# Second group of a fused attention and MoE kernel: half of its first product as seven half-size products, its second product in the later groups' order, and the early PSUM pool in two

## The chip, the cores and the metric

The kernel runs on one core of a Trainium2 chip. The metric is the device time of one execution in microseconds (us), as the median of several runs. The core's engines are PE (matrix products, with PEld for its weight loads), DVE (vector), ACT (scalar functions), POOL (GpSimd) and SP, which here only issues DMAs. Each engine works through its own queue in the order in which the kernel recorded its instructions, and semaphores order them against the other engines.

## The reference

```python
# 8 batches, 8 heads, 576 positions, head size 64
r = max(q, 0); q_p = [r*cos_w, r*sin_w]; k_p likewise          # features 128
kv = einsum('bhsf,bhsd->bhfd', k_p, v);  z = k_p.sum(axis=2)
x  = (einsum('bhsf,bhfd->bhsd', q_p, kv) / (einsum('bhsf,bhf->bhs', q_p, z) + 1e-6))
x  = x.transpose(0, 2, 1, 3).reshape(4608, 512)
h  = x @ w_in            # 512 x 2048, "product one"
g  = max(0.01 * h, h)
out = g @ w_out          # 2048 x 512, "product two"
```

## The kernel before, in words

The work is cut into nine groups of 512 tokens: groups 0 to 7 are the first 512 positions of a batch, group 8 gathers the last 64 positions of all eight. For each group the kernel prepares the features of q (`q_prep`, line 519, two instructions per call, one with the cosines and one with the sines) and of k (`k_cos`, `k_sin`, lines 456 and 459, one position out of nine and four heads' pairs at a time), copies v to 16 bits (`v_pairs`, line 477), forms kv on PE (`kv_sum`, line 490), transposes q's features (by PE for the first groups, by a DMA, `q_transpose_dma`, from group 2 on), forms the numerators (`num`, line 580), divides on DVE (`den`, `rec`, `mul`), transposes x (`x_transpose`, line 558, or a DMA), and then runs the two products.

**Product one.** Groups 0 and 1 do it directly (`ffn1`, line 622, called M or h): pairs of output tiles of 128 x 512 in a PSUM tile of two banks, four 512-column matmuls per tile, and one leaky ReLU of 1024 columns on ACT (line 644). From group 2 on it is done by Strassen's scheme in Winograd's form (`ffn1s` and `ffn1e`, lines 765 and 801): a group has four units u, each with seven products P(g,u,n) of four 256-column matmuls. A unit uses three PSUM banks, A, E and B, which rotate over four banks `ps_f` (`banks`, line 757). Its chain is: products 1 and 2 go to A, 5 and 3 to E, 6, 7 and 4 to B. After product 1 the step "b" copies A to B, after 5 the step "s" copies E to the one SBUF tile `s5`, product 6 adds to B, "w" writes E = B + s5 on DVE, products 3 and 7 may then go on, "y" writes y22 = B + s5 on DVE after product 7, and product 4 adds to B after "y". Steps a, c, e, d are the four leaky ReLUs on ACT (line 822). A capital B or S puts the copy on DVE, a small letter on ACT. The scheme needs sums of w_in (`w1_sum`, line 724) and, for each group, four sums of x (`x_sum`, line 741; X1, X2, X3, X4 each build on an earlier one).

**Product two.** All groups from 1 on use the same scheme for it (`ffn2s`, line 883, called F: 28 calls of four 256-column matmuls per group; group 7 goes one level deeper, line 1028). It needs sums of w_out (`weight_sum`, line 685) and of the activations G (`g_sum`, line 835). In the groups from 2 on the products run in the order 1, 6, 2, 7, 5, 4, 3 and accumulate into three chains in PSUM (`ORDER7`, `CHAIN`). Group 1 has an order and chains of its own (`ORDER71`, `CHAIN1`, line 875): products 2 and 4 get PSUM tiles of their own, so that `result` (line 922) adds on DVE what the later groups accumulate on PE.

**Order and buffers.** The order is written out by hand in the string `PROGRAM` (lines 25 to 163): each word is one call, in the order of recording, and its last letter is the engine (D, A or P). Every engine's queue follows from it. Capacity sets the rest: `stage` has four buffers for the loads, the pools `qpp` and `qpT` two each, kp one. PSUM is split into `ps_o` (two banks), `ps_n` (one tile of two banks) and, until the first Strassen unit, `ps_h` with two tiles of two banks (line 234). At the first call of `banks` the pool `ps_h` is closed and its four banks become `ps_f`. In the kernel before this happens at group 2; the PE transposes of x for group 2 still use a `ps_h` tile. `G7` = 1 names the first group with Strassen in product two, `F7` = 2 the first with it in product one.

Of the kernel before, what the change touches and what calls it, by code (L numbers as in the profile page):

```python
# [9 lines left out]
dt = mybir.dt  # L10
# [27 lines left out]
w1_sum(1,2,D) w1_sum(1,4,D) h(0,[14.15],[0.1.2.3],h) f2(1,0,4) f2(0,0,4) w2(2,P,2,4) q(1,0,0,8,D) weight_sum(2,0,4)  # L38
q(1,1,0,8,D) q(1,2,0,8,D) q(1,3,0,8,D) w2(2,D,0,2) k(1,0,1,c,D) k(1,0,1,s,D) k(1,1,2,c,D) k(1,1,2,s,D) v(1,0,1,D)
w2(3,D,2,4) f2(2,0,4) f2(0,4,8) f2(3,0,4) f2(2,4,8) qT(1,0,A,h) qT(1,1,A,h) f2(1,4,8) f2(3,4,8) qT(1,2,A,h) f2(1,8,12)  # L40
qT(1,3,A,h) f2(2,8,12) f2(0,8,12) v(1,1,2,A) kvps(1,h) kv(1,0,2) f2(3,8,12) kvo(1,0,2,A) w2(3,D,0,2)
k(1,2,4,c,A,[0.7]) v(1,3,4,A) k(1,2,4,c,D,[7.9]) nh(1,0,0,h) kvps(1,h) nh(1,1,0,h) f2(2,12,14) den(1,0,0) k(1,2,3,s,D)
rec(1,0,0) den(1,1,0) rec(1,1,0) k(1,3,4,s,D) mul(1,0,0) mul(1,1,0) load(k,3) load(q,3) f2(2,14,16) v(1,2,3,P)
f2(3,12,16) f2(0,12,16) kv(1,2,4) f2o(2,A) f2o(3,A) kvo(1,2,4,A) q_prep(2,0,0,8,A) f2o(0,A) xh(1,0,0,h) xh(1,1,0)
f2(1,14,15) nh(1,0,1,h) xho(1,0,D) nh(1,1,1,n) f2(1,12,14) h(1,[0.1],[0.1],h) den(1,0,1) den(1,1,1) rec(1,0,1)
mul(1,0,1) rec(1,1,1) mul(1,1,1) xh(1,0,1,o) xho(1,1,A,0,1) h(1,[2.3],[0.1],h) q_prep(2,2,0,8,D) k_sin(2,6,P)
xh(1,1,1) h(1,[4.5],[0.1],n) f2(1,15,16) xho(1,1,A,1,2) k_cos(2,8,A) f2o(1,A) h(1,[0.1.2.3.4.5],[2.3]) M(1,6) M(1,7)
M(1,8) M(1,9) M(1,10) k_cos(2,0,D) k_sin(2,4,D) q_prep(2,1,0,8,D) weight_sum(1,4,8) k_cos(2,2,D) k_cos(2,1,D)
q_prep(2,3,0,8,D) k_cos(2,5,P) k_cos(2,3,D) v_pairs(2,2,4,D) k_sin(2,8,D) k_sin(2,5,P) k_sin(2,3,P) w1_sum(0,3,D)
# [1311 lines left out]
```

## Time and profile before

| | |
|---|---|
| median of 3 runs | 269.49 us (269.48 to 272.55) |
| the profiled execution | 270.13 us |
| its span, first to last instruction | 268.1 us |
| granted TensorE clock | 1.00 throughout |
| DVE, ACT, POOL busy over the span | 83%, 69%, 42% |
| HBM read, written | 36.70 MB, 9.44 MB |

The span is 2.0 us shorter than the execution that it was taken from. In the profile, PE's instructions are pipelined: a 256-column matmul is shown with about 0.27 us although the next one starts 0.11 us later, so a busy share near 100% says only that PE always had something in its pipe. How fast it goes is read from the distance between the starts.

### The profile page before, as it was taken

Reading aid. Unit: us, or ns where it says so; the run is one execution under the profiler, and the core shown is the slowest. Engines: PE = TensorE matmul, PEld = TensorE weight load, DVE = VectorE, ACT = ScalarE, POOL = GpSimd, SP = SyncE. Lnnn points to the kernel's source line nnn. Section 1 sums busy time; section 2 is a strip of 40 time slices with the busy share of each in tenths; the row PEclk is TensorE's granted clock in tenths of the full one; section 3 lists DMA queues with packets and bytes.
Section 4 is the critical chain, followed back from the end, with each engine's and each line's share of the span. In section 5 each row is a group of like instructions: output and inputs, shape, how many; then the busy total and the mean of one; then the engine's idle time right before and its main releaser. Section 6 shows DMA issues by size and latency. Waiting matters only on the chain.

```text
span 268.1 us, 7401 instructions
## 1 busy us (share of the span) xinstructions
PE 261.7 (98%) x3009; PEld 223.1 (83%) x3009; DVE 222.9 (83%) x480; ACT 185.8 (69%) x336; POOL 113.5 (42%) x101
## 2 busy tenths in 40 slices
PE   8899999999999999999999999999999999999994
PEld 3675455656899999899999999999999999999983
DVE  4853899898989888799679799878798989998983
ACT  7866438778968988698896577886656376476610
POOL 2468011422838941090191369941461031354530
PEclk9999999999999999999999999999999999999999
DMA  7999999999999599979999899772756043100075
GB/s 231 363 394 412 382 398 373 391 255 210 265 241 348 108 243 208 366 174 247 238 325 182 141 355 250 180 111 51 142 134 143 18 76 122 41 0 2 2 236 156
DMA packets 75041, 57.09 MB, mean 213 GB/s; under 512 B 47232, under 2 KB 63616, under 8 KB 74624
## 3 DMA queue, kind: packets, MB, share of 16 engines
q1 hardware_dynamic: 74400, 56.11, 75.5%
q10 hardware_dynamic: 608, 0.52, 0.6%
q8 instruction: 23, 0.38, 0.5%
q14 instruction: 10, 0.08, 0.1%
HBM read 36.70 MB, written 9.44 MB: 172 GB/s over the span
## 4 chain that ended last, share of the span: by engine, by line
PE 85%; DMA 5%; ACT 4%; SPq 2%; POOL 1%; issue 1%; DVE 1%; ACTq 0%
PE ps_f L790 30%; PE ps L909 26%; PE ps_h L633 10%; PE ps_o L657 5%; DMA vst<-in_v_dram 3%; PE ps_kv L502 2%; PE ps L1061 2%; ACT qp L425 2%; DMA out_dram<-osb 2%; PE ps_num L586 2%; PE ps_y L1061 2%; PE ps_f L909 1%; SPq L539 1%; ACT vm L433 1%; PE ps_xT L1210 1%; PE ps_kv L1161 1%
## 5 line engine op out<-in xcount | busy, mean ns | idle before, releaser
L822 ACT ACTIVATE G<-ps_f 128x512 f16<-128x512 f32 x84 | 48.5, 597 | 30.5 <-PE ps_f L790 28.0
L909 PE MATMUL ps<-w,G 128*128 128x256 f16 x432 | 59.3, 273 | 0.0
L909 PEld LDWEIGHTS <-G 128*128 128x128 f16 x560 | 53.5, 98 | 5.6
L790 PE MATMUL ps_f<-xT,w 128*128 128x256 f16 x336 | 49.2, 273 | 0.0
L790 PEld LDWEIGHTS <-w 128*128 128x128 f16 x448 | 48.0, 114 | 0.9
L790 PEld LDWEIGHTS <-wsum 128*128 128x128 f16 x336 | 36.6, 114 | 0.9 <-issue 0.5
L909 PE MATMUL ps<-T,ext 128*128 128x256 f16 x208 | 29.6, 272 | 0.0
L633 PE MATMUL ps_h<-xT,w 128*128 128x512 f16 (+1 forms) x144 | 29.1, 355 | 0.0
L427 POOL TENSOR_SCALAR kp<-kst,sin_t 128x256 f16<-128x256 f32 x17 | 21.4, 1266 | 11.0 <-PE ps_kv L502 6.2
L790 PE MATMUL ps_f<-X,wsum 128*128 128x256 f16 x176 | 25.8, 273 | 0.0
L633 PEld LDWEIGHTS <-w 128*128 128x128 f16 x144 | 15.9, 114 | 10.9
L683 DVE TENSOR_TENSOR ps_f<-ps_f,s 128x512 f32<-128x512 f32 x28 | 19.5, 697 | 6.3 <-ACT s L433 3.8
L909 PEld LDWEIGHTS <-ext 128*128 128x128 f16 x224 | 21.4, 98 | 2.2
L644 ACT ACTIVATE G<-ps_h 128x1024 f16<-128x1024 f32 x16 | 15.9, 1022 | 7.2 <-PE ps_h L633 7.2
L683 DVE TENSOR_TENSOR y<-ps_f,s 128x512 f32<-128x512 f32 x28 | 19.2, 685 | 1.9 <-PE ps_f L790 1.5
L610 DVE TENSOR_TENSOR xs<-ps_num,rden 128x512 f16<-128x512 f32 x28 | 19.3, 688 | 0.7
L427 POOL TENSOR_SCALAR qp<-qst,cos_t 128x512 f16<-128x512 f32 (+1 forms) x5 | 9.5, 1892 | 23.6 <-DMA qpT<-qp 19.3
L822 ACT ACTIVATE G<-y 128x512 f16<-128x512 f32 x28 | 17.7, 632 | 0.8 <-DVE y L683 0.8
L433 ACT COPY ps_f<-ps_f 128x512 f32<-128x512 f32 x27 | 15.6, 579 | 3.1 <-PE ps_f L790 2.4
L790 PE MATMUL ps_f<-X,w 128*128 128x256 f16 x112 | 16.8, 273 | 0.0
L790 PE MATMUL ps_f<-xT,wsum 128*128 128x256 f16 x112 | 16.8, 273 | 0.0
L683 DVE TENSOR_TENSOR osb<-ps,ext 128x512 f32<-128x512 f32 x20 | 13.6, 683 | 2.3 <-PE ps L909 2.1
(171 smaller groups left out, 527.2 us busy)
## 6 DMA issues: line engine op xcount, KB each, us to landing
qst<-in_q_dram SPq DMA_DIRECT2D x7, 1024.0 KB, 10.2
out_dram<-osb SPq DMA_DIRECT2D x28, 256.0 KB, 4.6
kst<-in_k_dram SPq DMA_DIRECT2D x5, 1152.0 KB, 7.2
vst<-in_v_dram SPq DMA_DIRECT2D x5, 1152.0 KB, 9.0
w2st<-in_moe_w_out_dram SPq DMA_DIRECT2D x3, 1024.0 KB, 13.3
vst<-in_v_dram SPq DMA_DIRECT2D x4, 576.0 KB, 7.1
ext<-in_moe_w_in_dram SPq DMA_DIRECT2D x4, 512.0 KB, 11.2
kst<-in_k_dram SPq DMA_DIRECT2D x2, 576.0 KB, 7.8
```

What stands on the lines that cost most here:

```text
L425: nc.scalar.activation(o, i, AF.Relu, scale=col)
L427: eng.tensor_scalar(out=o, in0=i, scalar1=0.0, scalar2=col, op0=ALU.max, op1=ALU.mult)
L433: nc.scalar.copy(o, i)
L610: nc.vector.tensor_tensor(out=xs(), in0=ps[:, :, 0 : 4 * NE].rearrange("p a (b e) -> p a b e", e=NE)[:, :, :, 0:D], in1=st["rden", *k].rea ...
L633: nc.tensor.matmul(ps[:, m % 2, lo:hi], lhsT=w1[m // 4, c][0][:, w1[m // 4, c][1], m % 4 : 512 : 4], rhs=xT[:, lo // P : hi // P, c, :], s ...
L644: nc.scalar.activation(st["g", g][:, m - 1 : m + 1, :], ps, AF.Lrelu)
L657: nc.tensor.matmul(st["ps_o", g, tt], lhsT=st["g", g][:, m, tt * P : (tt + 1) * P], rhs=w2[:, m, :], start=(m == 0), stop=(m == NFT - 1),)
L683: eng.tensor_tensor(out=o, in0=a, in1=b, op=op)
L790: nc.tensor.matmul(ps[:, mi * HT : (mi + 1) * HT], lhsT=a[:, c, 2 * r0 + mi : 512 : 4], rhs=b[:, c], start=(n in (1, 5) and mi == 0 and c ...
L822: nc.scalar.activation(st["g", g][:, m : m + 2, r * HT : (r + 1) * HT], {"a": A, "c": y22, "e": E, "d": B_}[e].rearrange("p (m t) -> p m t ...
L909: nc.tensor.matmul(ps[:, tt], lhsT=a[:, i, tt * P : (tt + 1) * P], rhs=b[:, i], start=(first and i == 4 * halves[0]), stop=(i == NPR - 1 a ...
L1061: nc.tensor.matmul(ps, lhsT=a[:, i], rhs=b[:, i], start=(fresh and i == 0), stop=(i == NI - 1), skip_group_check=True,)
```

## The change

In group 1 the first half of product one (tiles 0 to 7, the calls `h`) stays direct. The second half, tiles 8 to 15 (`M(1,8)` to `M(1,15)`), becomes the units u = 2 and u = 3 of the Strassen scheme: P(1,2,n), P(1,3,n) with their steps e(1,2,.) and e(1,3,.). For these, x sums X1 to X4 of group 1 are formed (`x_sum(1,..)`), and the sums of w_in's second half are complete earlier (`w1_sum(1,3)`). `F7` is now compared with the running unit 4g + u, and is 6.

Product two of group 1 loses its own order and chains and takes those of the later groups: `R(1,2)` is a copy on ACT and no sum on DVE any more.

The pool `ps_h` becomes two pools of one tile each, chosen by a list of 26 digits (`H_BUF`), so that each half of the four `ps_f` banks takes the place of one of them. The transposes of x for group 2 write to two `ps_f` banks.

`PROGRAM` is written anew from the second group to the middle of group 4. The first difference comes after `f2(1,0,4) f2(0,0,4)`, from about unit 1 of group 4 on the words are nearly, and from `kv_sum(6,0,4,n)` on exactly, as before. In the new part the casts `w2(3,..)` of the last quarter of w_out move from DVE to ACT, `v(1,1,2)` from ACT to DVE, `v(1,3,4)` and `q_prep(2,1)` and more of `k_cos`/`k_sin` to POOL, and the loads `k(3)` and `q(3)` are recorded later.

```diff
-    F7 = 2
+    F7 = 6
...
-    early = ExitStack()
-    ps_h = early.enter_context(tc.tile_pool(name="ps_h", bufs=2, space=PS))
+    early = [ExitStack() for _ in range(2)]
+    ps_h = [
+        early[i].enter_context(tc.tile_pool(name=f"ps_h{i}", bufs=1, space=PS))
+        for i in range(2)
+    ]
+    taken = []
+    H_BUF = [int(i) for i in "01010110101010110100110101"]
...
-            early.close()
-            ps_f = pool("ps_f", 1, PS)
-            st["H"] = [ps_f.tile([P, 512], dt.float32, name=f"ps_f{i}") for i in range(4)]
+            for i in (1, 0):
+                early[i].close()
+            st["H"] = []
+            for i in range(2):
+                ps_f = pool(f"ps_f{i}", 1, PS)
+                st["H"] += [ps_f.tile([P, 512], dt.float32, name=f"ps_f{2 * i + j}") for j in range(2)]
...
-            st["ps_x", g] = psum("h", [P, 2, J // 2, NKC, P], dt.float16, "ps_x")
-        ps = st["ps_x", g][:, j % 2, j // 2]
+        ps = st["H"][(12 * g + 2 + j % 2) % 4].bitcast(dt.float16).rearrange(
+            "p (j c t) -> p j c t", j=J // 2, c=NKC
+        )[:, j // 2]
...
-    ORDER71 = (1, 2, 6, 5, 7, 4, 3)
-    CHAIN1 = {**CHAIN, 2: "W", 4: "V"}
...
-        lone, last = g == G7, g == NG - 1
-        order, chain = (ORDER71, CHAIN1) if lone else (ORDER79, CHAIN9) if last else (ORDER7, CHAIN)
+        last = g == NG - 1
+        order, chain = (ORDER79, CHAIN9) if last else (ORDER7, CHAIN)
```

The words of `PROGRAM` around the new units, before and after:

```diff
-xh(1,1,1) h(1,[4.5],[0.1],n) f2(1,15,16) xho(1,1,A,1,2) k_cos(2,8,A) f2o(1,A) h(1,[0.1.2.3.4.5],[2.3]) M(1,6) M(1,7)
-M(1,8) M(1,9) M(1,10) k_cos(2,0,D) k_sin(2,4,D) q_prep(2,1,0,8,D) weight_sum(1,4,8) k_cos(2,2,D) k_cos(2,1,D)
...
+h(1,[4.5],[2.3]) h(1,[0.1.2.3],[2.3]) f2(1,15,16) P(1,2,1) P(1,2,5) k_sin(2,5,D) e(1,2,b) k_sin(2,0,A) k_cos(2,8,P)
+k_cos(2,1,P) k_cos(2,6,A) x_sum(1,2,D) k_sin(2,4,P) k_sin(2,2,D) k_sin(2,3,A) h(1,[6.7],[0.1.2.3],n) weight_sum(4)
+k_cos(2,5,D) q_prep(2,3,0,8,D) k_sin(2,7,D) weight_sum(3) e(1,2,S) P(1,2,6) x_sum(1,4,D) e(1,2,w) P(1,2,2) P(1,3,1)
+e(1,2,a) x_sum(1,3,D) P(1,2,3) P(1,2,7) e(1,2,e) e(1,3,b) g_sum(1,1,0,4) e(1,2,y) P(1,3,5) g_sum(1,2,0,4) F(1,0)
+e(1,3,s) P(1,3,6) e(1,3,w) v_pairs(2,2,4,D) P(1,3,2) P(1,2,4) e(1,2,c) f2o(1,A) k_cos(2,0,A) k_cos(2,3,A) e(1,3,a)
+P(1,3,7) load(k,3) load(q,3) q_transpose_dma(2,0) P(1,3,3) F(1,2) k_cos(2,7,P) k_cos(2,4,P) k_sin(2,8,P)
+v_pairs(2,0,2,P) e(1,3,y) k_sin(2,1,D) q_prep(3,0,0,8,D) P(1,3,4) e(1,3,c) e(1,3,e) e(1,2,d) e(1,3,d) kv_sum(2,0,4,n)
```

How this moves the instructions, at three places. Rows read: line, operation, out<-in, shape; `xN` merges equal neighbours, "..." leaves rows out (on PE, the weight load ahead of every matmul and the other three matmuls of the same four). Lines of the changed kernel are some 10 to 20 higher: its 645 and 807 are 633 and 790 of the kernel before.

**PE, the second half of group 1's product one.** Before, where tiles 8 to 15 are made:

```order
L633 MATMUL ps_h<-xT,w_2_0_101 128x512
...
L633 MATMUL ps_h<-xT,w_2_2_102 128x512
...
L633 MATMUL ps_h<-xT,w_3_0_103 128x512
...
L633 MATMUL ps_h<-xT,w_3_2_104 128x512
...
L502 MATMUL ps_kv<-vm,kp 128x66
```

After, from the last of the direct tiles 6 and 7 on (933, 934, 938, 939 are the four banks; these rows are P(1,2,6), P(1,2,2), P(1,3,1), P(1,2,3), P(1,2,7), P(1,3,5)):

```order
L645 MATMUL ps_h<-xT,w_1_2_103 128x512
...
L807 MATMUL ps_f_938<-X_183,wsum 128x256
...
L807 MATMUL ps_f_933<-xT,w_2_2_105 128x256
...
L807 MATMUL ps_f_939<-xT,w_2_0_104 128x256
...
L807 MATMUL ps_f_934<-xT,wsum 128x256
...
L807 MATMUL ps_f_938<-xT,w_3_0_106 128x256
...
L807 MATMUL ps_f_933<-X1b,wsum 128x256
```

Between product 6 and product 3 of unit 2 stand three groups of four 256-column matmuls (product 6 itself, 2, and product 1 of unit 3), where before there were only direct tiles, which wait for no sum.

**ACT, the same place.** Before:

```order
L433 COPY osb<-ps_o 128x512
L644 ACTIVATE G_96<-ps_h 128x1024 x6
L425 ACTIVATE kp<-kst,cos_t 128x4x64 x2
L425 ACTIVATE kp<-kst,sin_t 128x4x64
L644 ACTIVATE G_96<-ps_h 128x1024 x2
L509 CAST kv_171<-ps_kv 128x2x4x66
```

After (the COPY rows are the steps b of units 2 and 3 and s of unit 3):

```order
L656 ACTIVATE G_99<-ps_h 128x1024 x3
L444 COPY ps_f_938<-ps_f_933 128x512
L436 ACTIVATE kp<-kst,sin_t 128x4x64
L436 ACTIVATE kp<-kst,cos_t 128x4x64
L436 ACTIVATE kp<-kst,sin_t 128x4x64
L656 ACTIVATE G_99<-ps_h 128x1024
L839 ACTIVATE G_99<-ps_f_933 128x2x256
L839 ACTIVATE G_99<-ps_f_934 128x2x256
L444 COPY ps_f_934<-ps_f_939 128x512
L444 COPY s_186<-ps_f_933 128x512
L839 ACTIVATE G_99<-y_187 128x2x256
```

Three leaky ReLUs of 1024 columns in a row now stand ahead of the first step of unit 2, and the second of them frees the tile whose banks product 1 of unit 2 writes.

**DVE, between the last division of group 1 and kv_sum of group 2.** Before:

```order
L427 TENSOR_SCALAR qp<-qst,cos_t 128x8x64
L427 TENSOR_SCALAR qp<-qst,sin_t 128x8x64
L683 TENSOR_TENSOR T_177<-w_105 128x1024
L427 TENSOR_SCALAR kp<-kst,cos_t 128x4x64 x2
L427 TENSOR_SCALAR qp<-qst,cos_t 128x8x64
L427 TENSOR_SCALAR qp<-qst,sin_t 128x8x64
L427 TENSOR_SCALAR kp<-kst,cos_t 128x4x64
L435 CAST vm<-vst 128x18x64
```

After (X1b, X_183 and X_184 are X1, X2 and X4 of group 1; the COPY is step s of unit 2, the row with ps_f_934 its step w):

```order
L695 TENSOR_TENSOR X_183<-xT,X1b 128x512
L438 TENSOR_SCALAR kp<-kst,sin_t 128x4x64
L695 TENSOR_TENSOR ext<-w_108,T_181 128x2048
L438 TENSOR_SCALAR kp<-kst,cos_t 128x4x64
L438 TENSOR_SCALAR qp<-qst,cos_t 128x8x64
L438 TENSOR_SCALAR qp<-qst,sin_t 128x8x64
L438 TENSOR_SCALAR kp<-kst,sin_t 128x4x64
L695 TENSOR_TENSOR w_108<-w_108 128x8x256
L446 COPY s_186<-ps_f_934 128x512
L695 TENSOR_TENSOR X_184<-xT,X_183 128x512
L695 TENSOR_TENSOR ps_f_934<-ps_f_938,s_186 128x512
L695 TENSOR_TENSOR xT<-xT 128x2x2x128
```

The steps s and w, for which PE waits, now stand behind two sums of 2048 columns, and the sum of x for product 7 (the last row) behind w.

More of the change, by code (lines that the diff above doesn't have):

```diff
@@ L742, in x_sum @@
         need(("xT", g), *(("X", g, i) for i in {1: (), 2: (1,), 4: (2,), 3: (1,)}[n]))
-        if g > F7 and n in (2, 4):
+        if g == 1 and n == 3:
+            need(*(("f1", 1, m) for m in range(8)))
+        if g > 1 and n in (2, 4):
             need(("f1", g - 1, "product", {2: 6, 4: 4}[n]))
@@ L1217, in xT_ho @@
         done.update(("xTc", b, 2 * hg + c, j) for c in range(*cs) for j in range(2 * lo, 2 * hi))
+        if all(("xTc", b, c, j) in done for c in range(NKC) for j in range(J)):
+            done.add(("xT", b))
         copy(
```

143 lines of the change are left out of this document (71 added, 72 removed).

## The prediction

> **What bounds the kernel now.** First the page, for which engine the end hangs on.
>
> ```profile
> PE 261.7 (98%) x3009; PEld 223.1 (83%) x3009; DVE 222.9 (83%) x480; ACT 185.8 (69%) x336; POOL 113.5 (42%) x101
> PE   8899999999999999999999999999999999999994
> PEclk9999999999999999999999999999999999999999
> PE 85%; DMA 5%; ACT 4%; SPq 2%; POOL 1%; issue 1%; DVE 1%; ACTq 0%
> ```
>
> PE has something in its pipe in every slice from the third to the last but one, at full granted clock, and the chain that ended last runs through it for 85% of the span. A time can come only out of the number of columns that PE passes, or out of holes between its matmuls. For these I read the timeline of PE around the change, by starts.
>
> ```profile
> 40.57 1.89 PE L657 MATMUL ps_o<-w,G 128*128 128x512 f16 x8
> 52.47 0.38 PE L657 MATMUL ps_o<-w,G 128*128 128x512 f16 x1
> 52.68 11.39 PE L633 MATMUL ps_h<-xT,w 128*128 128x512 f16 x52
> 64.00 1.32 PE L502 MATMUL ps_kv<-vm,kp 64*128 64x66 f16 x72
> ...
> 73.24 0.42 PE L586 MATMUL ps_num<-kv,qpT 128*128 128x66 f16 x8
> 73.72 0.38 PE L565 MATMUL ps_x<-ident,xs 128*128 128x128 f16 x4
> ...
> 92.55 0.60 PE L790 MATMUL ps_f<-X,w 128*128 128x256 f16 x4
> 92.99 0.60 PE L790 MATMUL ps_f<-xT,w 128*128 128x256 f16 x4
> 93.43 0.60 PE L790 MATMUL ps_f<-xT,wsum 128*128 128x256 f16 x4
> 93.86 0.60 PE L909 MATMUL ps<-w,G 128*128 128x256 f16 x4
> 94.43 0.60 PE L790 MATMUL ps_f<-X,w 128*128 128x256 f16 x4
> ...
> 109.87 0.42 PE L586 MATMUL ps_num<-kv,qpT 128*128 128x66 f16 x8
> 110.13 0.60 PE L909 MATMUL ps<-w,G 128*128 128x256 f16 x4
> 111.03 0.60 PE L790 MATMUL ps_f<-X1b,wsum 128*128 128x256 f16 x4 [0.30 <-ACT G L822]
> ```
>
> Eight 512-column matmuls take 1.89 us with a tail of 0.38 for the last: (1.89 - 0.38) / 7 = 0.216 us each. Four 256-column ones take 0.44 from start to start (92.55, 92.99, 93.43): 0.110 each. Against these rates there are three holes in the part that is written anew: 0.22 at 73.72 (eight num matmuls need 0.26, as from 109.87 to 110.13), 0.13 at 94.43, 0.46 at 111.03: together 0.81 us. The 52 direct matmuls run without one. The part of the kernel that is rewritten is thus nearly full, and PE bounds it.
>
> **The change part by part.** *Columns.* Tiles 8 to 15 cost 8 x 4 = 32 matmuls of 512 columns, 32 x 0.216 = 6.91 us. The two units cost 2 x 7 x 4 = 56 of 256 columns, 56 x 0.110 = 6.16. Gain **0.75 us**. Product two has 28 x 4 matmuls of 256 columns in either order, and kv, num and the transposes stay, so no other column is saved.
>
> *The wait of unit 2 for its banks.* Product 1 needs the tile of `h` 0 and 1 to be read by ACT. Tiles 4 and 5 are done first, then 0 and 1, then 2 and 3, in steps of four matmuls, 0.86 us; behind them comes one f2 matmul (0.22), then product 1. In the rows of the timeline and of the page
>
> ```profile
> 53.80 2.85 ACT L644 ACTIVATE G<-ps_h 128x1024 f16<-128x1024 f32 x3 [0.33 <-PE ps_h L633]
> ...
> L644 ACT ACTIVATE G<-ps_h 128x1024 f16<-128x1024 f32 x16 | 15.9, 1022 | 7.2 <-PE ps_h L633 7.2
> ```
>
> three leaky ReLUs take 2.85, of which one alone is 1.02 long, so they follow each other at 0.92. With the tail of the matmul (0.38 - 0.22 = 0.16) and a hand-over of 0.1, the first begins 0.26 after tiles 4 and 5, and the second ends at 0.26 + 0.92 + 1.02 = 2.20; PE reaches product 1 at 0.86 + 0.86 + 0.22 = 1.94. **+0.3 us**; bounds 0 (if the hand-overs cost nothing) and 0.6 (a k_sin of ACT in front is late by 0.3).
>
> *The chain inside the units.* What a step of the chain costs is shown at 92.99, where PE waits for y:
>
> ```profile
> 93.68 0.69 DVE L683 TENSOR_TENSOR y<-ps_f,s 128x512 f32<-128x512 f32 x1 [0.30 <-ACT kp L425]
> ```
>
> Product 7 starts at 92.99 and ends at 93.59, y runs from 93.68 to 94.37, product 4 starts at 94.43: 1.44 us from a product to the one that needs its sum, and PE was held up by it (the hole of 0.13). In the new order of PE twelve matmuls of 256 columns, 12 x 0.110 = 1.32, stand from product 6 to product 3 in unit 2, from 6 to 7 in unit 3, and from 7 to 4 in unit 3. Each lacks 0.12: **+0.4 us** with rounding. In the later groups other work stands between; here the only other work is eight matmuls of F(1,0) and F(1,2).
>
> *DVE ahead of step w.* The steps s and w of unit 2 stand behind the preparation of group 2.
>
> ```profile
> 50.95 0.48 DVE L427 TENSOR_SCALAR qp<-qst,cos_t 128x512 f16<-128x512 f32 x1
> 51.35 0.61 DVE L427 TENSOR_SCALAR qp<-qst,sin_t 128x512 f16<-128x512 f32 x1
> 51.88 0.56 DVE L427 TENSOR_SCALAR kp<-kst,cos_t 128x256 f16<-128x256 f32 x1
> 52.35 0.34 DVE L427 TENSOR_SCALAR kp<-kst,sin_t 128x256 f16<-128x256 f32 x1
> 52.62 0.62 DVE L427 TENSOR_SCALAR qp<-qst,cos_t 128x512 f16<-128x512 f32 x1
> 53.16 0.69 DVE L427 TENSOR_SCALAR qp<-qst,sin_t 128x512 f16<-128x512 f32 x1
> ...
> 59.23 1.21 DVE L683 TENSOR_TENSOR ext<-w,T 128x2048 f16<-128x2048 f16 x1
> 60.37 0.75 DVE L435 CAST vm<-vst 128x1152 f16<-128x1152 f32 x1
> ...
> 52.94 2.52 POOL L427 TENSOR_SCALAR kp<-kst,sin_t 128x256 f16<-128x256 f32 x2
> ```
>
> Beside POOL (busy here until 55.46) a half q takes 0.40 to 0.61 from start to start, say 0.52, and a k 0.27 to 0.47, say 0.37. A sum of 2048 columns takes 1.14 (59.23 to 60.37). From 51.1 on DVE has four halves of q (2.1), five k (1.85), two sums of x (0.35 each by the estimate of half a 1024-column sum, 0.7), two sums of 2048 (2.3) and then s (0.6, an estimate by half of the 1.21 above) and X4 (0.35): it is free for w at 59.0. PE comes to product 1 of unit 2 in the row order at 55.7 and ends product 6 at 55.7 + 0.44 + 0.44 + 8 x 0.216 + 0.60 = 58.9, so w could start at 59.0: **0 us**, but with no reserve. Bounds: 0, and 0.9 if every q and k goes at the slowest rate shown (0.61 and 0.47).
>
> *kv of group 1.* v(1,1) moves from ACT to DVE.
>
> ```profile
> 41.45 0.74 DVE L435 CAST vm<-ext 128x576 f16<-128x576 f32 x1
> 42.40 0.74 PE L1161 MATMUL ps_kv<-vm,kp 64*128 64x66 f16 x36
> ```
>
> DVE had its cast and one k (0.67) to 42.1; the second cast then ends at 42.85, while the second half of the 36 matmuls would start at 42.74: **+0.15 us** (bounds 0 and 0.4). In return ACT casts two quarters of w_out, which DVE does now:
>
> ```profile
> 42.11 1.28 DVE L435 CAST w<-ext 128x1024 f16<-128x1024 f32 x2
> ...
> 40.77 1.01 ACT L433 COPY qpT<-ps_qt 128x1024 f16<-128x1024 f16 x1 [0.25 <-PE ps_qt L575]
> ```
>
> No row shows ACT at it; the nearest is its copy of 1024 columns, 1.01, which I take (0.64 to 1.3 each otherwise, DVE's rate and POOL's 1.29 in the row further below). The second ends about 44.7, and f2 of these rows is reached at 45.0; it is hidden, and would cost what it is late beyond that.
>
> *Moved with cover.* R(1,2) becomes a copy on ACT for a sum on DVE, where ACT, with 8.36 us of 15.5 in the row of rival B, has room; the x transposes and product two's new chains have the same matmuls. On SP the loads of k(3) and q(3) keep their place in the queue; v(3)'s first half now stands between the two transposes of group 2's q, of which the second waits for q_prep(2,3) as the load does. More of k(2) is on POOL, whose work for group 2 I put at 12.5 us (11.71 in that same row, and a little more); from 47.4 on it ends near 60, before kv_sum(2) at about 64. All this costs nothing as long as these reserves stand.
>
> *Holes elsewhere.* The three holes of 0.81 us go with the old order; the new one up to group 4 is packed as closely, so I put in the same 0.81 for its own (bounds 0 and 2).
>
> Sum: -0.75 + 0.3 + 0.4 + 0 + 0.15 - 0.81 + 0.81 = **+0.1 us**: the span goes from 268.1 to 268.2. The profiled execution is 270.13 us and the median 269.49; the difference added to the median gives **269.6 us**.
>
> **The rivals.** *(A) The columns come through.* The waits in the units are hidden by what PE has queued, the holes of the old order vanish: -0.75 - 0.81 + 0.4 = -1.2, 268.3 us. For it speaks that the old order shows 52 matmuls without a hole and only 0.81 us in 50 us; against it, that the chain of 1.44 is longer than 1.32 on paper already.
>
> *(B) DVE takes over the bound in the new units (slower).* From the moment DVE reaches step w later than 59.0, each microsecond passes to PE undiminished, since eight matmuls (0.88 us) are all that does not depend on the units before kv_sum(2), which needs DVE's last k too. With 0.9 from the slow rates, 0.6 at the banks and 0.4 at kv, and 0.4 in the chain: -0.75 + 2.3 = +1.55, 271.0 us. DVE's 14.8 busy of 15.5 us in this stretch speak for it:
>
> ```profile
> 48.50:64.00 15.50, 15.50 (x92) 8.36 (x91) 14.84 (x34) 11.71 (x17) 4.93 (x4) 1.00 1.02 280
> ```
>
> against it, that w_out's last casts (1.28 us) leave DVE ahead of them and POOL takes three of the k and a q.
>
> *(C) POOL shuts DVE out.* One row shows a DVE instruction that waits for the whole of a POOL one:
>
> ```profile
> 35.90 1.29 POOL L435 CAST w<-w2st 128x1024 f16<-128x1024 f32 x1 [9.43 <-DMA w2st<-in_moe_w_out_dram]
> 36.20 1.26 DVE L427 TENSOR_SCALAR qp<-qst,sin_t 128x512 f16<-128x512 f32 x1
> ```
>
> 0.48 became 1.26. If each of the 13 DVE instructions ahead of s met this beside POOL's 12.5 us, at half of 0.8 to 1.2 each, w would be 6 us late: 269.6 + 6 = 275.6 us. Against it speaks that the six rows from 50.95 on, all beside POOL, lost some 0.8 us together, not 0.8 each. The Trainium skill ("SBUF — State Buffer", Who interferes with whom) states this as a rule: the port pair that DVE and GpSimd share is locked for the whole instruction, and the second one fully blocks. The trace agrees in the one row and not in the six.
>
> *(D) The columns saved don't reach the end*, because something else than PE sets it: then the time stays at 269.5 plus the waits only, 270.3. A PE at 98% leaves little room for it.
>
> **How the numbers follow.** Forecast, near balance, 0.55; A 0.22; B 0.16; C 0.03; D 0.04. The likeliest is 269.6 us. The range must hold A but for a little (to 268.2) and B with a worse packing later on (271.0 + 0.9 = 271.9); C and the rest of A lie outside: **268.2 to 271.9**. A change of 2% (5.4 us), about what a measurement of this kernel can tell from no change, would need on the fast side several times the 1.56 us that columns and holes hold: 0.01. On the slow side only C reaches it: 0.03. Within 2%: 0.96.
>
> **What would show it right or wrong.** Right: 24 more matmuls; product 1 of unit 2 some 0.3 us late behind the second leaky ReLU; 1.44 from product 6 to 3 in unit 2; DVE reaching w within 0.3 us of the end of product 6; kv of group 1 with a gap of 0.15 in its middle; from group 4 on the same distances as before. Wrong: a hole of over 1 us anywhere in PE between 50 and 130 us, above all ahead of product 3 of unit 2 (B or C), at kv_sum(2) (POOL or DVE late with k), or at num of group 2 (transposes late); or no hole at all in the units (A).

## The result, and the profile after

The changed kernel takes **271.8 us** (median of 20 runs, 270.52 to 273.1) against 269.73 us for the kernel before in the same sessions (20 runs). The ratio is **1.0061, 95% interval 1.004 to 1.0082**: slower by 1.1 to 2.2 us, far below 2%. The forecast was 269.6 us with a range of 268.2 to 271.9: the time lies 0.1 us inside the upper end, and a change of +0.1 us had been forecast where +2.1 came. The profiled execution took 272.29 us, its span is 270.5 us. The page, as before by engine and by the chain that ended last:

```profile
PE 261.5 (97%) x3033; PEld 225.1 (83%) x3033; DVE 226.2 (84%) x474; ACT 187.6 (69%) x341; POOL 133.2 (49%) x115
PE 77%; DMA 11%; DVE 6%; SPq 2%; issue 1%; ACT 1%; DVEq 0%
```

PE is busy as long as before (261.5 for 261.7) with 24 more, shorter matmuls, but the chain now runs through it for 77% and not 85%: 6% go through DVE and 11% through DMAs. POOL has 20 us more work. The units, in the timeline of PE:

```profile
55.20 0.38 PE L669 MATMUL ps_o<-w,G 128*128 128x512 f16 x1
55.71 0.60 PE L807 MATMUL ps_f<-xT,w 128*128 128x256 f16 x4
...
58.31 0.60 PE L807 MATMUL ps_f<-X,wsum 128*128 128x256 f16 x4
58.75 1.04 PE L807 MATMUL ps_f<-xT,w 128*128 128x256 f16 x8
59.86 0.60 PE L807 MATMUL ps_f<-xT,wsum 128*128 128x256 f16 x4
...
61.16 0.60 PE L919 MATMUL ps<-w,G 128*128 128x256 f16 x4
61.74 0.60 PE L807 MATMUL ps_f<-X,wsum 128*128 128x256 f16 x4
...
62.62 0.60 PE L807 MATMUL ps_f<-X,w 128*128 128x256 f16 x4
63.20 0.60 PE L807 MATMUL ps_f<-xT,w 128*128 128x256 f16 x4
...
64.07 0.60 PE L919 MATMUL ps<-w,G 128*128 128x256 f16 x4
64.63 0.60 PE L807 MATMUL ps_f<-X,w 128*128 128x256 f16 x4
```

Four matmuls of 256 columns need 0.44 from start to start, one of 512 needs 0.22; what is more is a hole. They are: 0.30 at 55.71 (product 1 of unit 2), 0.24 at 59.86 (product 3), 0.14 at 61.74 (product 6 of unit 3), 0.15 at 63.20 (product 7) and 0.13 at 64.63 (product 4), together 0.95 us, where the direct tiles had none. Further on there are 0.57 us at 72.74 (num of group 2) and 0.41 at 95.76 (product 1 of group 3).

The rest of the accounting uses four marks of PE that both programs share: an early matmul of group 1's product one (PE's number 470, counted from 0; before at 49.86, after at 50.01), the first matmul of kv_sum of groups 2 and 6, and PE's end. All values in us; "again" is the changed kernel profiled a second time.

| stretch | before | after | again |
|---|---|---|---|
| to matmul 470 | 49.86 | 50.01 | 49.96 |
| 470 to kv_sum 2 | 14.14 | 15.16 | 15.05 |
| kv_sum 2 to kv_sum 6 | 82.09 | 82.15 | 82.10 |
| kv_sum 6 to PE's end | 118.22 | 118.23 | 118.23 |
| PE's end to the span's end | 3.82 | 4.95 | 4.41 |

The second stretch of after holds eight more matmuls of product two (0.88), which its third stretch lacks. Taken together, 470 to PE's end is 1.09 us longer (0.93 again), the span's tail 1.13 (0.59 again). The part from kv_sum 6 on is the same to 0.02 us in all 14 profiles of this study. So there are two losses: one between 50 and 147 us, one behind PE's last matmul; 0.15 (0.10 again) stand ahead of matmul 470.

### The profile page after: what moved, and what is told of

It is laid out like the page before. It is cut to its first block, busy times and chain, and to the rows that moved or that the text cites. A ratio compares the mean times of both kernels' runs of the same rounds, so it can differ in the third digit from the quotient of the medians.

```text
span 270.5 us, 7473 instructions
## 1 busy us (share of the span) xinstructions
PE 261.5 (97%) x3033; PEld 225.1 (83%) x3033; DVE 226.2 (84%) x474; ACT 187.6 (69%) x341; POOL 133.2 (49%) x115
## 4 chain that ended last, share of the span: by engine, by line
PE 77%; DMA 11%; DVE 6%; SPq 2%; issue 1%; ACT 1%; DVEq 0%
PE ps_f L807 31%; PE ps L919 29%; DMA w2st<-in_moe_w_out_dram 5%; DMA w1st<-in_moe_w_in_dram 4%; PE ps_o L669 4%; PE ps_kv L513 3%; PE ps_num L598 3%; PE ps L1071 2%; DMA xT<-xs 2%; PE ps_y L1071 2%; PE ps_f L919 1%; DVE qp L438 1%; DVE kp L438 1%; SPq L314 1%; PE ps_qt L587 1%
## 5 line engine op out<-in xcount | busy, mean ns | idle before, releaser
L839 ACT ACTIVATE G<-ps_f 128x512 f16<-128x512 f32 x90 | 52.3, 596 | 32.8 <-PE ps_f L807 31.3
L807 PE MATMUL ps_f<-xT,w 128*128 128x256 f16 x360 | 52.1, 273 | 0.4 <-DMA xT<-xs 0.2
L807 PEld LDWEIGHTS <-wsum 128*128 128x128 f16 x360 | 39.1, 113 | 1.0 <-issue 0.2
L807 PE MATMUL ps_f<-X,wsum 128*128 128x256 f16 x184 | 27.1, 272 | 0.0
L438 POOL TENSOR_SCALAR kp<-kst,cos_t 128x256 f16<-128x256 f32 (+1 forms) x19 | 22.6, 1199 | 8.4 <-ACT G L839 4.4
L438 POOL TENSOR_SCALAR qp<-qst,cos_t 128x512 f16<-128x512 f32 (+1 forms) x7 | 14.0, 2007 | 24.3 <-DMA qpT<-qp 18.4
L695 DVE TENSOR_TENSOR ps_f<-ps_f,s 128x512 f32<-128x512 f32 x30 | 20.9, 695 | 5.7 <-ACT s L444 2.9
L645 PE MATMUL ps_h<-xT,w 128*128 128x512 f16 (+1 forms) x112 | 22.2, 348 | 0.0
L438 POOL TENSOR_SCALAR kp<-kst,sin_t 128x256 f16<-128x256 f32 x13 | 15.7, 1208 | 0.0
L656 ACT ACTIVATE G<-ps_h 128x1024 f16<-128x1024 f32 x12 | 11.9, 1023 | 5.5 <-PE ps_h L645 4.6
```

The source lines that it names most:

```text
L438: eng.tensor_scalar(out=o, in0=i, scalar1=0.0, scalar2=col, op0=ALU.max, op1=ALU.mult)
L645: nc.tensor.matmul(ps[:, m % 2, lo:hi], lhsT=w1[m // 4, c][0][:, w1[m // 4, c][1], m % 4 : 512 : 4], rhs=xT[:, lo // P : hi // P, c, :], s ...
L656: nc.scalar.activation(st["g", g][:, m - 1 : m + 1, :], ps, AF.Lrelu)
L695: eng.tensor_tensor(out=o, in0=a, in1=b, op=op)
L807: nc.tensor.matmul(ps[:, mi * HT : (mi + 1) * HT], lhsT=a[:, c, 2 * r0 + mi : 512 : 4], rhs=b[:, c], start=(n in (1, 5) and mi == 0 and c ...
L839: nc.scalar.activation(st["g", g][:, m : m + 2, r * HT : (r + 1) * HT], {"a": A, "c": y22, "e": E, "d": B_}[e].rearrange("p (m t) -> p m t ...
```

## The experiments

Theory H: the saved columns are paid back by local holes in the new order, each of which can be had back. Theory D: DVE with POOL beside it is full, so a hole that is closed opens again elsewhere. Expectations are quoted as they stood before each run. "470 to end" is the third and fourth marks' distance on PE: 214.45 us before, 215.54 and 215.38 after. This mark moves by some tenths from one profile to the next: before_pad, whose program is that of the kernel before up to 198 us, gives 214.04. A difference under 0.4 us is therefore read from the hole that went or came, and not from the mark alone. Diffs show words of `PROGRAM`; the numbers in brackets are the 95% interval of the ratio to the kernel before.

**again**: nothing altered.

> The changed kernel once more, nothing altered, for the spread and as the base of the others. Theory H (holes of the new order): the same holes in PE at the same places as in the first profile, 0.30 at product 1 of unit 2, 0.24 at its product 3, 0.57 at num of group 2, 0.41 at product 1 of group 3, and the end of PE 1.2 us later than before; the time 1.2 to 2.3 us above the kernel before. Theory J (the loss is a jitter of DMAs and of the output at the end): the holes stand elsewhere, and the end of PE is within 0.4 us of that of the kernel before.

Measured: 1.0069 (1.0045 to 1.0093). The holes stand at the same places (0.30, 0.14 at product 3, 0.14, 0.15, 0.13; 0.57; 0.50), PE ends 1.03 us later than before. The loss is no accident of one run; theory J is out for PE.

**bank**: PE gets other work while the banks come free.

```diff
-f2(1,15,16) P(1,2,1) P(1,2,5) ... h(1,[6.7],[0.1.2.3],n)
+f2(1,15,16) h(1,[6.7],[0.1],n) P(1,2,1) P(1,2,5) ... h(1,[6.7],[2.3],n)
```

> Four matmuls of tiles 6 and 7 are moved ahead of product 1 of unit 2, so that PE has 0.86 us of other work while the second leaky ReLU frees the banks. Theory H in its simple form: the 0.30 us hole goes and the end of PE comes 0.3 us earlier. Theory D: DVE reaches step w of unit 2 at the same time as now (it is busy until 0.2 us behind product 6 already), so product 3 starts where it started and its hole grows from 0.24 to some 0.54: no gain, under 0.1 us.

```profile
55.32 0.81 PE L645 MATMUL ps_h<-xT,w 128*128 128x512 f16 x3
55.97 0.60 PE L807 MATMUL ps_f<-xT,w 128*128 128x256 f16 x4
...
58.14 1.04 PE L807 MATMUL ps_f<-xT,w 128*128 128x256 f16 x8
59.15 0.60 PE L807 MATMUL ps_f<-xT,wsum 128*128 128x256 f16 x4
```

Product 1 follows the matmul ahead of it at once (three need 0.65), and the hole at product 3 did not grow: 59.15 - 58.14 - 0.88 = 0.13 (0.14 in again). From 470 to kv_sum 2 it takes 14.76 for 15.05 of again: the 0.30 is gained, theory H is right here. To PE's end it gains 0.65 in this one profile. The time does not show it: 1.0081 (1.0053 to 1.0108).

**bank_dve**: DVE's order ahead of the steps s and w of unit 2.

```diff
-weight_sum(3) e(1,2,S) P(1,2,6) x_sum(1,4,D) e(1,2,w) ... e(1,2,y)
+e(1,2,S) P(1,2,6) e(1,2,w) x_sum(1,4,D) ... e(1,2,y) weight_sum(3)
```

> As the run before it, and on DVE the sum of 2048 columns for product two (1.21 us) goes from ahead of steps s and w of unit 2 to behind step y, and the sum of x for product 4 from ahead of w to behind it. Theory D for this place (the new units wait for DVE's other work): w starts 0.1 us behind product 6, the bank hole and half of the hole at product 3 are gone: the end of PE 0.4 us earlier than in the changed kernel. Theory H without DVE: the same 0.3 us as the run before it brought, no more.

The timeline of DVE and PE around unit 3:

```profile
63.77 1.22 DVE L695 TENSOR_TENSOR w<-w 128x2048 f16<-128x2048 f16 x1
...
64.71 0.60 PE L807 MATMUL ps_f<-X,w 128*128 128x256 f16 x4
...
65.51 0.69 DVE L695 TENSOR_TENSOR ps_f<-ps_f,s 128x512 f32<-128x512 f32 x1
...
66.25 0.60 PE L807 MATMUL ps_f<-xT,w 128*128 128x256 f16 x4 [0.94 <-DVE ps_f L695]
```

Neither expectation held for PE's end. At unit 2, w does start 0.1 us behind product 6 (61.12 for 61.02), as theory D had it; but in bank, with the sum of 1.21 us still ahead of it, w also starts 0.1 us behind product 6 (58.40 for 58.30), so the sum had cost nothing there. Now it stands ahead of unit 3's w and makes that w 1.1 us late: product 7 starts at 66.25 where 65.15 would do. 470 to kv_sum 2 is 15.80, a microsecond more than bank. So it depends on the place what DVE can hide: the whole sum ahead of unit 2's w, next to nothing of it ahead of unit 3's. (This run also lost 2.7 us ahead of matmul 470, where no row differs from bank; its k tile landed at 9.53 us and not at 7.88. That part is not the experiment's, so the ratio, 1.014 (1.0113 to 1.0168), is no measure of it.)

**num_first**: two k features behind the division for which num waits.

```diff
-den(2,1) k_cos(3,1,D) k_sin(3,6,D) rec(2,1) mul(2,1)
+den(2,1) rec(2,1) mul(2,1) k_cos(3,1,D) k_sin(3,6,D)
```

> Two k features of group 3 on DVE are moved behind the reciprocal and the product of group 2's second quarter, for which num of the third quarter waits. Theory H: the 0.57 us hole ahead of that num shrinks to 0.1 or less and the end of PE comes 0.4 to 0.5 us earlier than in the unaltered changed kernel. Theory D (DVE as a whole is the bound): the k features come 1 us later, their wait turns up at kv_sum of group 3 or at the next division, and the end moves by less than 0.15 us. Theory J: no effect on the time beyond the spread.

In the changed kernel the features stand between `den` and `mul`, and num's tile is free only after `mul`:

```profile
70.65 0.15 DVE L608 TENSOR_SCALAR den<-ps_num 128x8 f32<-128x8 f32 x1
...
70.72 0.56 DVE L438 TENSOR_SCALAR kp<-G,cos_t 128x256 f16<-128x256 f32 x1
71.20 0.56 DVE L438 TENSOR_SCALAR kp<-G,sin_t 128x256 f16<-128x256 f32 x1
...
71.90 0.69 DVE L622 TENSOR_TENSOR xs<-ps_num,rden 128x512 f16<-128x512 f32 x1
...
72.74 0.41 PE L598 MATMUL ps_num<-kv,qpT 128*128 128x66 f16 x8 [0.40 <-DVE xs L622]
```

With them behind, that hole goes, and the next num waits 0.52 us:

```profile
75.16 0.43 PE L598 MATMUL ps_num<-kv,qpT 128*128 128x66 f16 x8 [0.35 <-DVE xs L622]
```

kv_sum 2 to kv_sum 3 is 13.08 for 13.04: theory D. 470 to end is 215.93, more than before the mend, and the ratio 1.008 (1.005 to 1.0109), because further on the mechanism of the prediction's rival C appeared:

```profile
115.44 2.24 POOL L446 CAST vm<-vst 128x1152 f16<-128x1152 f32 x2
...
115.64 2.58 DVE L695 TENSOR_TENSOR G<-G,ext 128x1024 f16<-128x1024 f16 x1
...
119.70 0.49 PE L807 MATMUL ps_f<-xT,w 128*128 128x256 f16 x3 [0.53 <-DVE ps_f L695]
```

A sum that takes 0.68 took 2.58: DVE came 0.2 us behind POOL and got nothing until both of POOL's casts were done. s, w and product 7 behind it were late, 0.70 us on PE. In again the same sum came 0.45 us ahead of the casts, and had its 0.68, although a feature was running on POOL from 0.64 us ahead of it to 0.50 behind its start:

```profile
115.78 0.68 DVE L695 TENSOR_TENSOR G<-G,ext 128x1024 f16<-128x1024 f16 x1
116.23 2.33 POOL L446 CAST vm<-vst 128x1152 f16<-128x1152 f32 x2
```

**num_act**: the two features leave DVE for ACT, a third goes behind a division.

```diff
-den(2,1) k_cos(3,1,D) k_sin(3,6,D) rec(2,1) mul(2,1) ... k_cos(3,8,D) mul(2,2) ... R(1,2,A)
+den(2,1) rec(2,1) mul(2,1) ... mul(2,2) k_cos(3,8,D) ... R(1,2,A) k_cos(3,1,A) k_sin(3,6,A)
```

> The two k features of group 3 that stood on DVE ahead of the division of group 2's second quarter go to ACT, into its idle 1.3 us there, and a third one on DVE goes behind the division of the third quarter. Theory D (DVE is the bound between kv_sum of group 2 and kv_sum of group 3, so that work must leave it): the hole of 0.57 at num goes and none of 0.5 takes its place as it did at the next quarter when the features were only put later; kv_sum of group 3 comes 0.45 to 0.6 us earlier. Theory H in its local form (each hole by itself): the same gain, but the next quarter shows its 0.5 us hole again, as no order of ACT's work bears on it.

```profile
72.31 0.42 PE L598 MATMUL ps_num<-kv,qpT 128*128 128x66 f16 x8
...
74.97 0.42 PE L598 MATMUL ps_num<-kv,qpT 128*128 128x66 f16 x8
```

Measured: no hole at either num (the rows name no wait); kv_sum 2 to kv_sum 3 is 12.44 for 13.04, 470 to end 214.51, and 1.0057 (1.0031 to 1.0084). Theory D: putting DVE's work later brought nothing, taking it off DVE brought 0.60. Between matmul 470 and PE's end this kernel is now as fast as the one before (214.45), and its time is still 1.5 us longer: in its profile, what is left of the span's loss lies ahead of matmul 470 (0.39) and behind PE's end (0.63).

**p30**: other products fill the hole ahead of product 1 of group 3.

```diff
-P(3,0,1) ... P(2,3,4) P(3,0,5) ... P(3,0,6) ... F(2,1) F(2,2) P(3,1,1)
+P(2,3,4) P(3,0,1) ... P(3,0,5) F(2,2) ... P(3,0,6) ... F(2,1) P(3,1,1)
```

> Product 4 of the last unit of group 2 is put ahead of product 1 of group 3, and a product-two step of four matmuls behind product 5 of group 3. Theory H (the hole of 0.31 to 0.50 there is the landing of group 3's x transpose): product 4 fills most of it; what is left is 0.2 ahead of product 4 (step y ends 0.3 behind the matmul ahead), and the end of PE comes 0.2 to 0.35 us earlier. Rival (the x transpose is not what PE waits for): a hole of 0.3 to 0.5 stands again ahead of product 1 or product 6 of group 3, no gain.

What PE waits for there, in the chain of waits of the changed kernel, is the DMA of group 3's x transpose:

```profile
89.08 0.49 ACT s L444
89.57 0.01 issue
89.58 6.14 DMA xT<-xs
95.72 0.05 issue
95.76 0.30 PE ps_f L807
```

And with the products moved:

```profile
94.73 0.60 PE L919 MATMUL ps<-w,G 128*128 128x256 f16 x4
95.30 0.60 PE L807 MATMUL ps_f<-X,w 128*128 128x256 f16 x4
95.73 0.60 PE L807 MATMUL ps_f<-xT,w 128*128 128x256 f16 x4
...
98.35 0.60 PE L807 MATMUL ps_f<-xT,w 128*128 128x256 f16 x4
99.29 0.60 PE L807 MATMUL ps_f<-xT,w 128*128 128x256 f16 x4 [0.34 <-DVE ps_f L695]
```

The hole shrank to 0.13, ahead of product 4, and product 1 of group 3 (95.73) follows with none: the x transpose was what PE waited for, against the rival. But a hole of 0.50 opened at 99.29, behind step w, where the filler had been taken from. 470 to end is 215.54: no gain, as the rival had it, for another reason than the rival's. The ratio was 1.0118 (1.0065 to 1.0171, four runs).

**direct** and **direct2**: the units alone undone.

```diff
-P(1,2,n) P(1,3,n) e(1,2,.) e(1,3,.) x_sum(1,n,D) ... w1_sum(1,3,D)
+M(1,8) M(1,9) ... M(1,14) M(1,15) ... w1_sum(1,3,D) behind kv_sum(2,0,4,n)
-F7 = 6
+F7 = 8
```

> The units alone undone: in the changed kernel, tiles 8 to 15 of group 1 are direct again (32 matmuls of 512 columns, leaky ReLUs of 1024 columns on ACT, no x sums and no steps of group 1), all else of the change stays: product two in the later order, the split PSUM pools, the work moved between engines. Measured at the end of PE against the changed kernel. Theory H (columns gained are paid back by the stalls inside the units): columns +0.81, the stalls inside the units of 0.65 go, the wait of 0.30 for the first bank stays with the first direct tile: +0.15, between -0.1 and +0.4. Theory D (the units' cost is their 5 us of DVE, which make num of group 2 and the k features late): the hole of 0.57 at num of group 2 closes as well, -0.4. Theory A (the saved columns come through, the loss is only in the rest): +0.8.

> The units alone undone, as in the run named direct, but with the copy and two k features on ACT ahead of the last pair of direct tiles in ACT's queue; there they stood behind its leaky ReLU, and kv_sum of group 2 waited 1.7 us for them. From PE's matmul 470 to its end, against 215.4 in the changed kernel: theory H (columns +0.81, stalls inside the units -0.65): 215.4 to 215.7, no difference worth a measurement; theory A (the columns of the units come through): 216.1 or more; theory D (the units' DVE work is what makes num late): 214.8 or less.

In direct, kv_sum 2 waited 1.7 us for k features that I had left behind a leaky ReLU on ACT, so it tells nothing of the units (1.0105, 1.0076 to 1.0134). In direct2 470 to end is 215.71, 0.2 to 0.3 more than with the units: within theory H, but no more than the mark moves by itself. Its time is 1.0056 (1.0036 to 1.0076), not to be told from the changed kernel's. Three larger holes stand in it, without any unit (0.30, 0.68 and 0.54 us):

```profile
55.10 0.38 PE L669 MATMUL ps_o<-w,G 128*128 128x512 f16 x1
55.61 7.07 PE L645 MATMUL ps_h<-xT,w 128*128 128x512 f16 x32
...
68.71 1.05 PE L919 MATMUL ps<-T,ext 128*128 128x256 f16 x8 [0.52 <-DVE ext L695]
...
73.44 0.41 PE L598 MATMUL ps_num<-kv,qpT 128*128 128x66 f16 x8 [0.37 <-DVE xs L622]
```

The first is the bank wait, now ahead of the first direct tile: it belongs to the order and not to the units. The second is direct2's own: the sum `w1_sum(1,3)`, put back behind kv_sum 2, stands on DVE ahead of the sum that product two waits for. So the units are best read up to kv_sum 2, ahead of both other holes: 15.31 us for 15.16 (15.05 again). The units gain 0.15 to 0.25 there, which is their columns (0.81) less the holes in their chain (0.66, 0.55).

**direct_num**: direct2 with the words of num_act.

> As direct2, and the k features moved as in num_act. Theory H: the same 0.6 to 0.9 us as num_act brought to the changed kernel: 214.6 to 215.0 from matmul 470 to the end, and since this kernel has so few ACT instructions that none is the 448th, the span ends 3.8 us behind PE; time 0.3 to 0.9 us above the kernel before. Rival (the hole at num comes from the units): the gain is under 0.3.

Measured: 215.19 (0.52 less than direct2; kv_sum 2 to kv_sum 3 takes 13.13 for 13.70) and 1.0035 (1.0018 to 1.0052), the lowest of the changed kernels. The gain is a little under H's 0.6 and above the rival's 0.3: the hole at num does not come from the units. Against num_act, which has the units and the same mend at num, PE's part is 0.68 longer (215.19 for 214.51), as much as the hole that direct_num keeps from direct2 (0.68), and the tail 0.66 shorter (3.79 for 4.45).

**pad** and **before_pad**: the tail.

```diff
+pad=lambda n: [nc.scalar.activation(warm, zero, AF.Lrelu) for _ in range(n)],
+pad(12) qT(1,2,A,h)
```

in pad, and in the kernel before

```diff
-e(6,2,c)
+e(6,2,c) pad(9)
```

> The changed kernel with 12 ACT instructions on one column each, in an idle time of ACT about 38 us, so that every later ACT instruction stands 12 further in the program. In the four profiles with the changed program's ACT queue the last output DMA on ACT is issued 0.35 to 0.40 us after the semaphore it waits for, against 0.07 in the kernel before, and the span ends 4.4 us or more behind PE against 3.8. Theory F (a block of ACT's program ends just there and the next has to come): with the shift, the gap of 0.4 goes from the last output DMA and the span ends 0.3 to 0.4 us sooner behind PE; the time 0.3 us lower. Theory E (the wait is for the output DMAs themselves): the gap stays at 0.35 to 0.40 and the end too.

> The kernel before with 9 one-column ACT instructions in an idle time of ACT at about 198 us and nothing else, so that its last output DMA becomes ACT's row 447, as it is in the changed kernel. Theory F (the start of ACT's 448th instruction costs 0.3 us, wherever it falls): the last output DMA is issued 0.33 us after its semaphore instead of 0.07 and the span ends 4.1 to 4.4 us behind PE instead of 3.8; time +0.3 us. Theory E (the gap belongs to the changed program): 0.07 and 3.8, time unchanged within 0.1.

ACT issues two output DMAs at the end. In the rows below (first of the kernel before, then of again, pad and before_pad) the group's time less the two issues is the gap between them; a second view gives the issues as 0.585 and 0.535, 0.790 and 0.492, 0.808 and 0.587, 0.564 and 0.492.

```profile
264.09 1.25 ACTq L1111 DMA_DIRECT2D out_dram<-osbl  x2
```

```profile
265.12 1.68 ACTq L1121 DMA_DIRECT2D out_dram<-osbl  x2
```

```profile
266.58 1.49 ACTq L1121 DMA_DIRECT2D out_dram<-osbl  x2
```

```profile
263.34 1.47 ACTq L1111 DMA_DIRECT2D out_dram<-osbl  x2
```

The gaps are 0.13, 0.40, 0.10 and 0.41. Theory F, as far as the position goes: the kernel before gets the gap of the changed one by nine one-column instructions, and the changed one loses it by twelve. Counted with semaphore rows and DMA issues, the last output DMA is ACT's row 438 before, 447 after; in all eight profiles where row 447 (of a count from 0) is an output DMA, it starts 0.33 to 0.35 us behind the row ahead of it; in the six others the last output DMA starts 0.04 to 0.09 behind. The tail is 4.34 us in before_pad for 3.82, and 4.00 in pad for 4.41. In time before_pad is at 1.0009 (0.9992 to 1.0027), which neither shows nor excludes 0.3 us. pad's own 1.009 (1.0064 to 1.0116) holds more: ACT was not idle where I put the twelve, and kv of group 1 and the num behind it show holes of 0.53 and 0.59 (matmul 470 at 50.80).

**mended**: bank, num_act and ten pads together, two matmuls of tile 6 and 7 behind product 6, and `x_sum(1,4,D)` behind `e(1,2,w)`.

> The changed kernel with the mends together: four matmuls of tiles 6 and 7 ahead of product 1 of unit 2 and two behind product 6, the sum of x for product 4 behind step w, two k features of group 3 on ACT, one behind a division, and 10 one-column ACT instructions in an idle time at about 198 us, so that ACT's row 447 no longer falls on an output DMA. Theory H (the loss is the sum of local holes, each of which can be had back): the bank hole, the hole at product 3 and the one at num go; from PE's matmul 470 to its end 214.0 to 214.4 us, where the changed kernel took 215.4 to 215.5 and the kernel before 214.45; the span ends 3.8 us behind PE; the time within 0.3 us of the kernel before, against 1.7 to 2.0 above it unmended. Rival (the holes turn up again, as in two of the runs ahead): 215 or more, and a time 1 us or more above the kernel before.

```profile
60.02 1.04 DVE L695 TENSOR_TENSOR X<-xT,X 128x512 f16<-128x512 f16 x1
...
61.44 0.60 PE L807 MATMUL ps_f<-xT,w 128*128 128x256 f16 x4 [0.69 <-DVE xT L695]
```

The bank hole and the ones at num are gone, as in the single runs; the one at product 3 is not (0.22). But the sum of x behind w took 1.04 for 0.41 (POOL was casting from 59.63 on), so the sum behind it was late, and product 7 of unit 2 waited 0.85 us; another 0.56 opened at 133 us. 470 to end is 215.93: the rival. 1.0054 (1.0026 to 1.0081).

The tail was not mended either: the gap between ACT's last two DMAs is down to 0.08, but PE's end to the span's end takes 4.36. The last output DMA starts 0.49 us behind PE's end, as in the kernel before, and lands 0.56 later than there. So the tail does not follow the gap alone. It is 3.79 to 3.82 us in the four profiles whose ACT queue ends ahead of row 447 (before, direct, direct2, direct_num) and 4.00 to 4.95 in the ten others; what lengthens it there beside the gap is open. No version beats the kernel before.

## Why the prediction was right, and where it was not

The forecast of 269.6 us missed by 2.2 us. The time lies in the range because its upper end had been set for rival B and 0.9 us of worse packing together. The worse packing came (0.8 us), B did not, and a longer tail, which had no term, stands in its place: that the number fell inside is luck. What the prediction had right is the account of the units; what it had wrong stands outside them. By its own steps, with the first profile (again in brackets where it differs):

| term | forecast | measured |
|---|---|---|
| columns | -0.75 | -0.81 (56 x 0.109 for 32 x 0.216) |
| bank wait of unit 2 | +0.3 | +0.30 |
| chain in the units | +0.4 at three places | +0.66 at four (0.55) |
| DVE ahead of w | 0, up to 0.9 | 0.1, in the 0.24 at product 3 (0) |
| kv of group 1 | +0.15 | +0.13, in the middle of its 36 matmuls |
| old holes | -0.81 | -0.81 (-0.36 in before_pad) |
| new holes elsewhere | +0.81, up to 2 | +1.6 |
| behind PE | not considered | +1.13 (0.59) |
| sum | +0.1 | +2.2 (+1.5), of +2.4 (+1.6) in the span |

The **mechanism** held where the new units are: the columns come through, and the wait for the banks and the chain (1.55 us from product 6 to product 3, 1.44 again) pay them back. These three terms make +0.15 us (+0.04 again) for a forecast of -0.05. direct2 shows the same up to kv_sum 2, and that the bank wait stays without the units. The chain was a little underrated, since it has a fourth place: P(1,3,6) at 61.74 waits for the copy b of unit 3, which writes the bank of E of unit 2 and so stands behind step e.

*DVE ahead of w* was put at 0 with no reserve, from rows:

```profile
57.05 1.21 DVE L695 TENSOR_TENSOR w<-w 128x2048 f16<-128x2048 f16 x1
58.19 0.68 DVE L446 COPY s<-ps_f 128x512 f32<-128x512 f32 x1
58.79 0.41 DVE L695 TENSOR_TENSOR X<-xT,X 128x512 f16<-128x512 f16 x1
59.12 0.68 DVE L695 TENSOR_TENSOR ps_f<-ps_f,s 128x512 f32<-128x512 f32 x1
```

w starts at 59.12 (forecast 59.0), 0.21 behind product 6, which ends at 58.75 + 0.16. Some 0.1 us is lost there (the sum of x ahead of it ends at 59.20), nothing in again. So rival B's mechanism is out in the new units as they are, though its 271.0 us is the nearest of the named values; bank_dve shows it at unit 3's w as soon as DVE gets something more there (1.1 us).

The step that failed is **"holes elsewhere"**: "the new one up to group 4 is packed as closely, so I put in the same 0.81". It holds 1.6: 0.57 at num of group 2, 0.41 at the x transpose of group 3, and 0.15, 0.15, 0.17 and 0.17 at 82.61, 94.05, 99.45 and 139.96. The order on PE told how closely its rows follow each other, not what DVE has to do between them; two k features between `den` and `mul` were to be seen in DVE's order, and I had followed that engine only to kv_sum 2. And over half of the old holes was luck of the phase: before_pad, the same program but for nine instructions at 198 us, lacks the 0.46 at 111 us.

The **tail** was missing from the sum. In again it is 0.59 longer than before. Of this, 0.27 is the gap ahead of ACT's last DMA (0.40 for 0.13), which pad and before_pad show to hang on the position; the other 0.3, in longer issues and the landing of the output, stays open, and mended shows that the tail can be as long without the gap. In the first profile it is longer by another 0.54, with one ACT issue of 1.82 us

```profile
263.68 1.82 ACTq L1135 DMA_DIRECT2D out_dram<-osb  x1
```

for 0.65 in before and again; why is open as well.

Rival A (268.3) is out: the columns are paid back. Rival C in its size is out, but its mechanism is shown by num_first: 1.9 us in one place. In pad the same sum took 2.49. The Trainium skill ("SBUF — State Buffer", Who interferes with whom) states that a DVE instruction with two inputs in SBUF and a GpSimd instruction that reads SBUF exclude each other, and that the one issued second waits for the whole of the first. The rows agree in part. Of DVE's sums of 128 x 1024 in the fourteen profiles, 27 start while POOL is casting, and 26 of these take 0.75 to 2.58 us for 0.68. But 132 start while POOL prepares features, which also read SBUF, and 100 of them take under 0.72 (POOL's own spans are rough in a profile). In num_first and pad two casts back to back held DVE for both; in p30, where the same sum came 0.69 us behind the first cast, it took 1.00, less than the rest of the first cast (0.45) and its own time together, so the second cast did not hold it there.

That 1.9 us more or less hang on under 0.7 us of phase (0.45 ahead of the casts in again, 0.2 behind in num_first) may be why the changed kernel, with 133 us of POOL for 113, spreads over 270.5 to 273.1 us where most runs of the kernel before lie within 269.3 to 270.6. This is argued, not tried: no experiment took POOL's work away. Open, too, is the start: matmul 470 came between 49.5 and 50.8 us (52.4 in bank_dve).

## What to carry to other kernels

A saving in columns on an engine that is full is worth what its new waits leave of it: price the longest chain from one product to the next against the work that stands between, bank reuse included, and follow the helping engine (DVE here) as far as the order is new. Closing one hole by putting its work later moved it; taking the work to another engine closed it; and several mends at once brought new collisions. A mark over a long stretch moves by some tenths by itself, so read an experiment from the hole that it was made for. Look behind the last matmul as well: the end of the program is on the path whatever PE does.

## What the runs showed of the hardware that was not expected

- In the eight profiles, of seven programs, where ACT's row 447 is an output DMA, it starts 0.33 to 0.35 us behind the row ahead of it, where the last output DMA of the six others takes 0.04 to 0.09. That a block of ACT's program ends there, as theory F has it, is argued from the position alone. In the other profiles row 447 either waits for PE or does not exist, so they show nothing of it.
- The tail behind PE's end was 3.79 to 3.82 us in the four profiles whose ACT queue ends ahead of row 447, and 4.00 to 4.95 in the ten others.
- A DVE sum of 128 x 1024 took 2.58 us for 0.68 when it came 0.2 us behind two POOL casts, and 0.68 when it came 0.45 us ahead of them. POOL's features held such a sum far less often than its casts (32 of 132 took 0.72 us or more, 26 of 27).
- Two programs with the same rows up to 50 us (bank and bank_dve) differed by 2.7 us at matmul 470 in their profiles; their first k tile landed at 7.88 and at 9.53 us.
